# Two head pairs' start-up work put in another order: the first pair's maxima, their turn and two scores ahead of the second pair's join, casts and maxima, with six filling products instead of sixteen

## The chip, the cores and the metric

The kernel runs on one core of one Trainium2 chip. The metric is the device time of one execution in microseconds (us); less is better. A core has five engines that run side by side and wait for each other through semaphores: TensorE (PE in the profile, with PEld for its weight loads), VectorE (DVE), ScalarE (ACT), GpSimd (POOL) and SyncE (SP), which issues the transfers (DMA).

## The reference, cut to what matters

```python
q_rot, k_rot = (rotate(q), rotate(k))            # 8 batches, 8 heads, 576 rows, 64 columns
scores = scale * np.matmul(q_rot, k_rot.transpose(0, 1, 3, 2))
scores = scores - np.max(scores, axis=-1, keepdims=True)
attn = np.exp(scores)
attn = attn / (np.sum(attn, axis=-1, keepdims=True) + 1e-09)
x = np.matmul(attn, v)                           # heads side by side: 4608 x 512
logits = x @ phi                                 # a soft mixture of 8 experts, 32 slots, follows
...
```

Attention for 64 heads comes first; its output goes through a mixture of experts in which every slot is a softmax-weighted mean over all rows. The change touches attention alone.

## The kernel before

**Pairs.** Two heads make a pair, `p` or `q` in the code, and there are 32. For each pair the same steps are run, and each step has a name:

- `load0.p`, `load1.p`: transfers of the pair's q and k into a tile `x_in`, of which there are two. `spin0.p`, `spin1.p` (L237, POOL): products with cosine and sine. `join.p` (L244, DVE): the sum that ends the rotation.
- `high1.p`, `high0.p` (L250, ACT): casts of the rotated k and q to 16 bits, into the tile `hl`; `low.p` (L254, DVE): what the cast left over, also 16 bits. `low.p` is the last reader of the pair's `x_in`, so `load0.p+2`, which uses the same buffer, waits for it.
- the maxima: `m00.p` to `m31.p` are eight units of two products each of the casts (L296, PE), each into a PSUM bank, with a row maximum behind it (L298, DVE); `m_rem.p` is the ninth (L305 and L307). A unit of pair 0 has two more products, which only keep PE busy (L293). `m_min.p` (L320 and L322, DVE) joins the two halves.
- the turn: for pairs 0 and 1, `m_rows.p` is `m_lay` (L346 and L348, PE: six products with an identity matrix, then L349, ACT, which writes the row `peak`). Later pairs do it with transfers.
- the scores: `t0.p` to `t7.p` (L372, PE: eight products, the last two of which subtract `peak`; then L373, ACT: the exponential), `t8.p` for the rest, and `av0.p` to `av4.p` (L407, PE), which multiply by v.

**Banks.** Four double banks of PSUM (`s_ps0` to `s_ps3`) go round. A step takes the one that was given back longest ago; its first product waits until DVE or ACT has read what lay there.

**Order.** Every engine runs its instructions in the order in which the program issues them. At the start of the kernel that order is written out by hand, in a list of names `FRONT`; behind it come tables of times. Ahead of `FRONT` pair 0's rotation, its casts and 21 filling products (`heat`, L724) are issued. `heat.0` in `FRONT` is one more run of 16 filling products; they read the casts of pair 0, go into a bank that nobody reads, and serve only to keep PE busy.

Of the kernel before, what the change touches and what calls it, by code (L numbers as in the profile page):

```python
# [84 lines left out]
    3.879855, 5.365764), "bs3": 34.500363, "bs4": 35.968859, "bs5": 43.198227, "bs6": 50.043832,  # L85
}
FRONT = (
# [70 lines left out]
def attn_softmoe(ctx, tc, qk, v, phi, w1, w2, cs, ident, sel, seg, out):  # L158
# [109 lines left out]
    def bank2(k=None):  # L268
        if k is None:
            k = min((i for i in range(N_S) if age[i] is not None), key=lambda i: age[i])  # L270
        age[k] = None
        t = ps[k].tile([P, 2, 512], F32, name=f"s_ps{k}")
        held[id(t)] = k, t
        return t

    def free(t):
        k, _ = held.pop(id(t))
        age[k] = next(ages)
# [441 lines left out]
    def heat(n):  # L720
        cold = bank2()
        free(cold)
        for _ in range(n):
            nc.tensor.matmul(cold[:, 0, 0:HC], lhsT=lift, rhs=halves[0][:, KH, 0:HC], start=True, stop=True)  # L724

    def small_loads(p):
# [1 line left out]
        nc.sync.dma_start(out=sel_sb, in_=sel)  # L728

    plan.update({  # L730
        "heat": lambda p: heat(16),
        "small_loads": small_loads,
        "join0": lambda p: join(p, 0),
        "join1": lambda p: join(p, 1),
# [332 lines left out]
```

## Time and profile before

| | |
|---|---|
| median of 3 runs | 479.99 us (479.64 to 480.94) |
| the profiled execution's own time | 480.02 us |
| its span, first to last instruction | 478.2 us |
| busy: PE, PEld, DVE, ACT, POOL | 96%, 78%, 77%, 60%, 60% |
| mean granted clock of TensorE | 0.993 |

Every time below is counted from the start of the span. A busy share is a mean over the whole span; the change lies in the first 30 us, so the stretch from 14 to 28 us has to be read by itself. PE's records are pipelined and overlap: the distance from one start to the next tells more than a duration. [...]

### The profile page before, as it was taken

To read this page: it belongs to the slowest core of one execution; us is meant where nothing else is said; L and a number is where in the kernel's file an instruction comes from. 1 tells how busy PE (TensorE), PEld (TensorE's weight loads), DVE (VectorE), ACT (ScalarE), POOL (GpSimd) and SP (SyncE) were. 2 spreads that over 40 slices of the span, in tenths; PEclk is the share of its full clock that TensorE was granted. 3 is DMA by queue.
4 is the path that set the end of the run, shared out by engine and by line. 5 is a ranking of instruction groups with operands and counts; after the bars stand their busy time and mean duration, and the time that the engine had idled before them with its cause. 6 is when DMAs were issued, how large, how long until landed. Compare 5 with 4: busy or idle time off the path is not lost.

```text
span 478.2 us, 24158 instructions
## 1 busy us (share of the span) xinstructions
PE 458.3 (96%) x10787; PEld 371.5 (78%) x10787; DVE 366.3 (77%) x616; ACT 285.7 (60%) x656; POOL 288.0 (60%) x319
## 2 busy tenths in 40 slices
PE   4799999999999999999999999999999999989993
PEld 2487888878888888878887888888888888853762
DVE  5989998888878887998899789988896864263242
ACT  2156767675667567657765676577766766530242
POOL 4886958848783888488856886687749302120000
PEclk9899999999999999999999999999999999999998
DMA  7444845473655355446533653346352044799997
GB/s 280 172 166 176 269 153 197 164 261 102 202 175 213 110 201 174 120 145 210 171 113 123 250 172 125 149 139 217 126 191 112 15 181 163 237 382 407 408 370 319
DMA packets 28795, 93.97 MB, mean 196 GB/s; under 512 B 5012, under 2 KB 5396, under 8 KB 28692
## 3 DMA queue, kind: packets, MB, share of 16 engines
q1 hardware_dynamic: 28692, 92.44, 54.1%
q8 instruction: 84, 1.38, 1.2%
q14 instruction: 19, 0.16, 0.1%
HBM read 82.92 MB, written 9.44 MB: 193 GB/s over the span
## 4 chain that ended last, share of the span: by engine, by line
PE 91%; DVE 4%; ACT 2%; DMA 1%; issue 1%; SPq 0%; DVEq 0%; ACTq 0%
PE s_ps L407 33%; PE s_ps L372 26%; PE s_ps L296 8%; PE s_ps L387 4%; PE o_ps L927 3%; PE o_ps L903 3%; PE s_ps L480 2%; PE s_ps L517 2%; PE c_ps L950 2%; DVE nm L298 2%; PE s_ps L724 2%; PE s_ps L305 2%; PE s_ps L577 1%; DVE hl L254 1%; DMA x_in<-in_qk 1%
## 5 line engine op out<-in xcount | busy, mean ns | idle before, releaser
L237 POOL TENSOR_TENSOR x_in<-x_in,cs_sb 128x288 f32<-128x288 f32 x248 | 236.2, 986 | 79.5 <-DMA x_in<-in_qk 62.5
L298 DVE TENSOR_REDUCE nm<-s_ps 128x2 f32<-128x576 f32 x256 | 187.3, 752 | 50.0 <-PE s_ps L296 48.8
L407 PEld LDWEIGHTS s_ps<-v_in,a_t 128*64 128x64 f32 x4608 | 139.3, 137 | 12.4 <-issue 4.8
L373 ACT ACTIVATE a_t<-s_ps 128x576 f32<-128x576 f32 x256 | 146.0, 658 | 3.6 <-PE s_ps L372 3.1
L407 PE MATMUL s_ps<-v_in,a_t 128*64 128x66 f32 x4608 | 146.4, 222 | 0.2 <-issue 0.2
L372 PE MATMUL s_ps<-hl 64*128 64x288 f16 x1536 | 133.1, 283 | 0.4 <-DVE nm L307 0.2
L372 PEld LDWEIGHTS <-hl 64*128 64x128 f16 x1536 | 79.3, 94 | 18.5 <-issue 8.0
L372 PE MATMUL s_ps<-peak,lift 64*128 64x288 f16 x512 | 75.3, 283 | 0.3 <-ACT peak L349 0.3
L296 PE MATMUL s_ps<-hl 64*128 64x288 f16 x512 | 66.8, 286 | 0.7 <-ACT a_t L373 0.4
L438 ACT COPY o_sb<-s_ps 128x528 f32<-128x528 f32 x31 | 18.6, 601 | 74.9 <-PE s_ps L407 74.9
L456 POOL TENSOR_TENSOR xn<-o_sb,rr 128x640 f32<-128x640 f32 x31 | 41.0, 1332 | 31.7 <-PE s_ps L577 13.9
L254 DVE TENSOR_TENSOR hl<-x_in,hl 128x1152 f16<-128x1152 f32 x32 | 53.7, 1678 | 1.6 <-ACT hl L250 1.6
L250 ACT CAST hl<-x_in 128x576 f16<-128x576 f32 (+1 forms) x66 | 40.9, 659 | 20.5 <-DVE x_in L244 20.4
L244 DVE TENSOR_TENSOR x_in<-x_in 128x1152 f32<-128x1152 f32 (+1 forms) x35 | 46.2, 1321 | 0.1
L296 PEld LDWEIGHTS <-hl 64*128 64x128 f16 x512 | 29.0, 94 | 15.6 <-issue 6.8
L372 PEld LDWEIGHTS <-lift 64*128 64x128 f16 x512 | 27.0, 94 | 4.9 <-issue 0.5
L407 PE MATMUL s_ps<-v_in,a_tr 64*64 64x66 f32 x1152 | 26.4, 224 | 0.0
L307 DVE TENSOR_REDUCE nm<-s_ps 128x2 f32<-128x576 f32 x32 | 24.0, 749 | 2.5 <-PE s_ps L305 2.5
L407 PEld LDWEIGHTS s_ps<-v_in,a_tr 64*64 64x64 f32 x1152 | 21.9, 133 | 4.3 <-issue 3.5
L387 PE MATMUL s_ps<-hl 64*64 64x256 f16 (+1 forms) x384 | 23.9, 286 | 0.0
L962 DVE COPY w_exp<-c_ps 128x512 f32<-128x512 f32 x16 | 10.3, 686 | 17.3 <-PE c_ps L950 14.6
L500 ACT COPY xt<-s_ps 128x576 f32<-128x576 f32 x31 | 19.2, 650 | 5.0 <-PE s_ps L480 5.0
(174 smaller groups left out, 409.2 us busy)
## 6 DMA issues: line engine op xcount, KB each, us to landing
x_in<-in_qk SPq DMA_DIRECT2D x61, 576.0 KB
w_exp<-in_w SPq DMA_DIRECT2D x53, 512.0 KB
v_in<-in_v SPq DMA_DIRECT2D x32, 330.0 KB
out<-w_exp SPq DMA_DIRECT2D x18, 512.0 KB
wt<-in_w SPq DMA_DIRECT2D x11, 512.0 KB
peak<-mr SPq DMA_DIRECT2D x120, 0.5 KB
x_in<-in_qk SPq DMA_DIRECT2D x4, 288.0 KB
cs_sb<-in_cs SPq DMA_DIRECT2D x2, 288.0 KB
```

Of the source, the lines that this page charges most:

```text
L237: eng.tensor_tensor(out=run_on(x[:, c]), in0=run_on(x[:, c]), in1=run_on(cs_sb[:, c]), op=ALU.mult)
L244: nc.vector.tensor_tensor(out=x[:, :, 0], in0=x[:, :, 0], in1=x[:, :, 1], op=ALU.add)
L250: nc.scalar.copy(out=out, in_=loaded[p][:, t, c, 0])
L254: nc.vector.tensor_tensor(out=hl[:, 0:4:3], in0=x[:, :, :, 0], in1=hl[:, 1:3], op=ALU.subtract)
L296: nc.tensor.matmul(s[c, h, 0:HC], lhsT=hl[rows[h], QH, P * j + c.start:P * j + c.stop], rhs=hl[rows[h], KH, half[n]], start=True, stop=True)
L298: nc.vector.tensor_reduce(out=nm[:, n, j:8:4], in_=s[:, :, 0:HC], axis=AX.X, op=ALU.max, negate=True)
L307: nc.vector.tensor_reduce(out=nm[:, :, 8], in_=s[:, :, 0:HC], axis=AX.X, op=ALU.max, negate=True)
L372: nc.tensor.matmul(s[c, h, 0:HC], lhsT=lhs, rhs=rhs, start=(x == 0), stop=(x == 3))
L373: nc.scalar.activation(out=ats[p, b][:, :, half[n]], in_=s[:, :, 0:HC], func=AF.Exp, scale=SCALE)
L387: nc.tensor.matmul(s[rows[h ^ n], n, 0:w] if n else s[rows[h], 0, 512 - w:512], lhsT=lhs, rhs=rhs, start=(x == 0), stop=(x == 3))
L407: nc.tensor.matmul(o[rows[c], h, VW * u:VW * u + VW], lhsT=lhs, rhs=v, start=(i == 0 and u == 0), stop=(left_av[p] == 0 and u == 3 + (c == ...
L456: eng.tensor_tensor(out=xn, in0=t[:, :, :, 0:64], in1=rr.unsqueeze(3).broadcast_to([P, 2, 5, 64]), op=ALU.mult)
```

## The change

In `FRONT` the steps `join.1` and `high1.1` move behind `m_min.0`, `heat.0` and `m_rows.0`, together with `high0.1` and `bs1.2` (which issues nothing at this place), and `t5.0`, `t7.0` move ahead of `m30.1` and `m11.1`. The number of products in `heat.0` goes from 16 to 6.

```diff
-    "logits.0 m11.0 m31.0 low.0 m00.0 spin0.1 spin1.1 m30.0 m20.0 m21.0 m10.0 join.1 m_rem.0 m01.0 load0.2 "
-    "high1.1 m_min.0 heat.0 high0.1 bs1.2 m30.1 m11.1 spin0.2 m_rows.0 low.1 t5.0 t7.0 weights.7 m31.1 t4.0 "
+    "logits.0 m11.0 m31.0 low.0 m00.0 spin0.1 spin1.1 m30.0 m20.0 m21.0 m10.0 m_rem.0 m01.0 load0.2 "
+    "m_min.0 heat.0 m_rows.0 join.1 high1.1 high0.1 bs1.2 t5.0 t7.0 m30.1 m11.1 spin0.2 low.1 weights.7 m31.1 t4.0 "
...
-        "heat": lambda p: heat(16),
+        "heat": lambda p: heat(6),
```

Behind this place `FRONT` goes on as before: `load_v.1 load1.2 t6.0 m20.1 t1.0 m21.1 spin1.2 load0.3 m10.1 join.2 t0.0 t3.0 ...`. The orders of POOL and SP are the same in both.

ACT's queue, from the end of pair 0's casts to the first exponentials (`hl_151` is pair 0's, `x_in_143` pair 1's), before:

```order
L250 CAST hl_151<-x_in_136 128x288 x4
L250 CAST hl_245<-x_in_143 128x576 x2
L349 ACTIVATE peak0_105<-s_ps2_280 128x576
L373 ACTIVATE a_t_289<-s_ps3_290 128x2x288
L373 ACTIVATE a_t_300<-s_ps0_301 128x2x288
```

and with the change:

```order
L250 CAST hl_151<-x_in_136 128x288 x4
L349 ACTIVATE peak0_105<-s_ps0_253 128x576
L250 CAST hl_262<-x_in_143 128x576 x2
L373 ACTIVATE a_t_265<-s_ps1_266 128x2x288
L373 ACTIVATE a_t_276<-s_ps2_277 128x2x288
```

`peak` of pair 0 now stands ahead of the two casts of pair 1.

DVE's queue, from the last of pair 0's plain maxima (into `nm2_184`) to pair 1's third (pair 1's are `nm2_267` before, `nm2_287` with the change), before:

```order
L298 TENSOR_REDUCE nm2_184<-s_ps0_224 128x2
L244 TENSOR_TENSOR x_in_143<-x_in_143 128x8x144
L307 TENSOR_REDUCE nm2_184<-s_ps1_231 128x2
L298 TENSOR_REDUCE nm2_184<-s_ps2_237 128x2
L320 TENSOR_REDUCE cn_sb_114<-nm2_184 128x2x4
L322 TENSOR_REDUCE cn_sb_114<-nm2_184 128x2
L298 TENSOR_REDUCE nm2_267<-s_ps0_268 128x2
L298 TENSOR_REDUCE nm2_267<-s_ps1_272 128x2
L254 TENSOR_TENSOR hl_245<-x_in_143,hl_245 128x2x576
L298 TENSOR_REDUCE nm2_267<-s_ps1_313 128x2
```

and with the change:

```order
L298 TENSOR_REDUCE nm2_184<-s_ps0_224 128x2
L307 TENSOR_REDUCE nm2_184<-s_ps1_230 128x2
L298 TENSOR_REDUCE nm2_184<-s_ps2_236 128x2
L320 TENSOR_REDUCE cn_sb_114<-nm2_184 128x2x4
L322 TENSOR_REDUCE cn_sb_114<-nm2_184 128x2
L244 TENSOR_TENSOR x_in_143<-x_in_143 128x8x144
L298 TENSOR_REDUCE nm2_287<-s_ps3_288 128x2
L298 TENSOR_REDUCE nm2_287<-s_ps0_292 128x2
L254 TENSOR_TENSOR hl_262<-x_in_143,hl_262 128x2x576
L298 TENSOR_REDUCE nm2_287<-s_ps1_303 128x2
```

The join (L244) moved behind the last maxima of pair 0 and their minima; nothing else moved.

PE's queue with the change, one row of each step, from the filling products to `t1.0` (weight loads and a step's other products are left out; the row into `s_ps1_303` is `m31.1`, the last is `t1.0`):

```order
L724 MATMUL s_ps3_246<-hl_151,lift_101 128x288
...
L346 MATMUL s_ps0_253<-id_sb_96,cn_sb_114 128x128 x4
...
L372 MATMUL s_ps1_266<-hl_151 128x288
...
L372 MATMUL s_ps2_277<-hl_151 128x288
...
L296 MATMUL s_ps3_288<-hl_262 128x288
...
L296 MATMUL s_ps0_292<-hl_262 128x288
...
L296 MATMUL s_ps1_303<-hl_262 128x288
...
L372 MATMUL s_ps2_307<-hl_151 128x288
...
L372 MATMUL s_ps3_320<-hl_151 128x288
...
L296 MATMUL s_ps0_330<-hl_262 128x288
...
L372 MATMUL s_ps1_335<-hl_151 128x288
```

Before, the two rows into `s_ps3_288` and `s_ps0_292` (`m30.1` and `m11.1`) stood ahead of the turn (L346). Behind `m31.1` the order is the same in both, and in both `t1.0` goes into the bank that `m31.1` used (`s_ps1`).

## Rows read from the trace of the kernel before

**Rows 1.** The page: busy time of each engine (part 1), chain by engine (part 4).
```profile
PE 458.3 (96%) x10787; PEld 371.5 (78%) x10787; DVE 366.3 (77%) x616; ACT 285.7 (60%) x656; POOL 288.0 (60%) x319
...
PE 91%; DVE 4%; ACT 2%; DMA 1%; issue 1%; SPq 0%; DVEq 0%; ACTq 0%
```

**Rows 2.** Waits of PE from 46 to 420 us: total us, times, longest.
```profile
PE s_ps L372 <- DVE nm L307: 0.2, 1, 0.2
```

**Rows 3.** Timeline of PE, 17 to 28 us: start, us, what, [idle before].
```profile
17.14 3.65 PE L724 MATMUL s_ps<-hl,lift 128*128 128x288 f16 x16 [0.24 <-DVE nm L298]
20.71 0.52 PE L296 MATMUL s_ps<-hl 64*128 64x288 f16 x4
21.16 1.16 PE L346 MATMUL s_ps<-id_sb,cn_sb 128*128 128x128 f32 x8
...
23.33 0.30 PE L372 MATMUL s_ps<-peak,lift 64*128 64x288 f16 x2 [0.27 <-ACT peak L349]
...
23.94 0.30 PE L296 MATMUL s_ps<-hl 64*128 64x288 f16 x2
...
25.16 0.55 PE L372 MATMUL s_ps<-hl 64*128 64x288 f16 x6
...
26.68 0.55 PE L372 MATMUL s_ps<-hl 64*128 64x288 f16 x6
```

**Rows 4.** Timeline of DVE, 14 to 25.5 us.
```profile
14.35 3.40 DVE L298 TENSOR_REDUCE nm<-s_ps 128x2 f32<-128x576 f32 x5
17.67 1.34 DVE L244 TENSOR_TENSOR x_in<-x_in 128x1152 f32<-128x1152 f32 x1
18.94 0.74 DVE L307 TENSOR_REDUCE nm<-s_ps 128x2 f32<-128x576 f32 x1
19.60 0.74 DVE L298 TENSOR_REDUCE nm<-s_ps 128x2 f32<-128x576 f32 x1
...
20.47 0.15 DVE L322 TENSOR_REDUCE cn_sb<-nm 128x2 f32<-128x4 f32 x1
21.15 1.42 DVE L298 TENSOR_REDUCE nm<-s_ps 128x2 f32<-128x576 f32 x2 [0.53 <-PE s_ps L296]
22.49 1.58 DVE L254 TENSOR_TENSOR hl<-x_in,hl 128x1152 f16<-128x1152 f32 x1
24.28 0.76 DVE L298 TENSOR_REDUCE nm<-s_ps 128x2 f32<-128x576 f32 x1 [0.21 <-PE s_ps L296]
```

**Rows 5.** Timeline of ACT, 18.5 to 25 us.
```profile
19.05 1.24 ACT L250 CAST hl<-x_in 128x576 f16<-128x576 f32 x2 [7.53 <-DVE x_in L244]
22.63 0.65 ACT L349 ACTIVATE peak<-s_ps 128x576 f16<-128x576 f32 x1 [2.34 <-PE s_ps L348]
23.66 1.75 ACT L373 ACTIVATE a_t<-s_ps 128x576 f32<-128x576 f32 x3 [0.39 <-PE s_ps L372]
```

**Rows 6.** PE by window: stretch, length, PE busy (instructions), granted clock, DMA share, GB/s.
```profile
14.10:17.10 3.00, 1.28 (x12) 1.00 0.56 161
17.54:20.94 3.40, 3.40 (x18) 0.50 0.99 387
20.95:23.00 2.05, 2.05 (x22) 1.00 0.16 57
```

**Rows 7.** Timeline of SP's queue: issues of `x_in` transfers, 13 to 36 us.
```profile
15.77 9.17 SPq L232 DMA_DIRECT2D x_in<-in_qk  x3
```

**Rows 8.** Timeline of POOL, 13 to 40 us: the products of pair 3.
```profile
28.04 7.76 POOL L237 TENSOR_TENSOR x_in<-x_in,cs_sb 128x288 f32<-128x288 f32 x8 [1.81 <-DMA x_in<-in_qk]
```

**Rows 9.** Timeline of DVE, 36 to 43.7 us: the join of pair 3, and a wait.
```profile
37.11 1.35 DVE L244 TENSOR_TENSOR x_in<-x_in 128x1152 f32<-128x1152 f32 x1
...
41.16 0.17 DVE L326 TENSOR_REDUCE min<-nm 128x9 f32<-128x18 f32 x1
41.49 1.92 DVE L254 TENSOR_TENSOR hl<-x_in,hl 128x1152 f16<-128x1152 f32 x1 [0.16 <-ACT hl L250]
43.34 0.20 DVE L334 STREAM_TRANSPOSE turned<-min 128x32 f32<-128x32 f32 x1
```

## The prediction

> **What bounds the kernel now.** I read the page first. PE is busy for 96% of the span, and the chain of work that ended last runs over PE for 91% [rows 1]. Busy PE records overlap and prove little alone, so next I asked what PE waits for once the start is over: between 46 and 420 us there are just two waits in the list, of 0.2 us each (the other is a wait for issue) [rows 2]. So PE has no reserve there that could take up a delay. What PE loses or gains before 30 us should stand in the end time, and the question is only when PE gets through the stretch that the change rearranges.
>
> There I read the three timelines side by side. PE runs 16 filling products from 17.14 until `m30.1` follows at 20.71, then turns pair 0's maxima (L346) at 21.16, and `t1.0` comes at 25.16 [rows 3]. DVE has hardly any gap: five maxima until 17.67, the join of pair 1, the last two maxima of pair 0, the minima, 0.53 idle, then two maxima of pair 1 and `low.1` until 24.07, and the maximum of `m31.1` at 24.28 [rows 4]. ACT makes pair 1's casts from 19.05 to 20.29, then idles for 2.34 until the turn is done [rows 5]. The reader should see two chains: PE to ACT to PE (turn, `peak`, scores) for pair 0, and DVE to ACT to PE to DVE (join, casts, products, maxima, `low.1`) for pair 1. They meet at the bank of `m31.1`, which `t1.0` takes next. Its maximum ends at 24.28 + 0.76 = 25.04, and `t1.0` starts at 25.16 [rows 3, 4]: pair 1's chain has about 0.1 us to spare.
>
> [...]
>
> **The change part by part.**
>
> *The turn comes earlier.* Nothing changes on DVE until 17.67. Without the join there, the maximum of `m_rem.0` starts at 17.67, that of `m01.0` 0.66 later (19.60 - 18.94), at 18.33, and the second minimum 0.87 after it (20.47 - 19.60), from 19.20 to 19.35 [rows 4]. Handing over to PE takes about 0.05, as from `peak` (22.63 + 0.65 = 23.28) to 23.33 [rows 3, 5]. So the turn starts at 19.40 instead of 21.16.
>
> *Ten fills go.* Sixteen took 20.71 - 17.14 = 3.57, or 0.22 each; six end at about 18.5 [rows 3]. PE then waits 0.9 us for the minima, so these ten cost or give nothing by themselves: what is late next is the turn's input.
>
> *The turn at the lower clock.* From the turn's first product to `peak` it took 22.63 - 21.16 = 1.47 at a granted clock of 1.00 [rows 3, 5, 6]. At 19.40 the clock stands at 0.50 if it falls and rises as before; PE's work ahead of 17 us is the same. Then 1.54 us until 20.94 do half as much, 0.77, and 0.70 remain: `peak` starts at 21.64 and ends at 22.29. Bounds: 20.87 for its start with a full clock throughout, 22.34 with half throughout. The first I call 0.77 early, the second 0.70 late.
>
> *The casts wait behind `peak`.* The join now starts at about 19.28 and ends at 20.62 (1.34 long) [rows 4]. ACT is free then, and casts followed the join within 0.05 before (17.67 + 1.34 = 19.01, and 19.05) [rows 4, 5]. But `peak` stands ahead of them in ACT's queue. ACT starts one instruction of this size 0.55 after another ((1.75 - 0.65) / 2), so the casts start at 21.64 + 0.55 = 22.19, and end 1.24 later, at 23.43 [rows 5]. This is the new wait: 1.5 us in which ACT holds ready work.
>
> That the queue doesn't let a ready instruction pass is shown on DVE: a minimum ended at 41.16 + 0.17 = 41.33, the transpose that reads only it ran at 43.34, behind a `low` that waited for ACT [rows 9]. [...]
>
> *Pair 1's chain.* `m30.1` then starts at 23.48 and its maximum 0.34 later (23.94 to 24.28 for `m31.1`), at 23.82, against 21.15 before [rows 3, 4]. DVE idles for 3.2 us instead of 0.53. Two maxima and `low.1` take until 24.07 - 0.07 (DVE starts the next some 0.07 before an end: 17.67 + 1.34 against 18.94), so 2.85; `m31.1`'s maximum runs from 26.67 to 27.43, and `t1.0` starts at 27.48 instead of 25.16: 2.3 us late [rows 3, 4]. The two scores done early don't help: PE reaches `t1.0` and stands still.
>
> *What may be won back.* From `m31.1` to `t1.0` PE took 25.16 - 23.94 = 1.22 for two units and two scores, and 26.68 - 25.16 = 1.52 for the next two units and two scores, so 0.30 there was waiting [rows 3]; ACT's exponentials are earlier now, but `t3.0` must wait for `t1.0`'s. Between 0 and 0.3 comes back; I take 0.1, as its bank is the nearer wait.
>
> *SP and POOL.* `low.1` frees the tile for `load0.3`, which SP holds among the three issues from 15.77 to 24.94 [rows 7]. It comes 2.67 later, and POOL's products of pair 3 with it: they end at 38.5 instead of 28.04 + 7.76 = 35.80 [rows 8]. `join.3` started at 37.11 and would now be due at 39.3, so this is covered by 0.8 [rows 9]. Uncovered, it would cost 0.45.
>
> **Sum:** +2.3 - 0.1 = +2.2 us. From the profiled execution's own 480.02 us (the median of the runs is 479.99, practically the same) that is **482.2 us**, +0.46%. A change of 0.3% (1.44 us) is about what a measurement of this kernel can tell from none. With the clock's bounds: 481.4 to 482.9.
>
> **The rivals.**
>
> *The clock falls again* (slower still). PE gets `m31.1` at about 24.0 (after the first exponential), two scores and a unit until about 25.7, and then stands until 27.48: some 1.5 us of work in 4. The clock fell before after 1.28 of 3.00 [rows 6]. If it is at 0.50 for 3.40 us again, at most half of that is lost, 1.7; part of it lies behind DVE, so 1.1: 483.3, at most 483.9. For more than 0.20 I would need a second such stretch in the rows. Chance 0.20.
>
> *The clock doesn't fall before the turn.* Then +1.4, 481.4, at the edge of what can be told. The runs of before lie 1.3 us apart, so executions differ. Against it: PE's work ahead is unchanged. Chance 0.13.
>
> *The delay is taken up later.* 480.0. [...] Chance 0.06.
>
> *ACT runs the casts first.* They would end at 20.66 + 1.24 = 21.90, maxima start at 22.29 instead of 23.82, `t1.0` is 0.8 late: 480.8. Chance 0.02, by rows 9.
>
> *Faster.* Pair 0's chain alone decides: the turn starts 1.76 earlier, so 478.3. It holds if `t1.0` isn't held by `m31.1`'s bank; for that the casts must end 2.3 us earlier than I find, by 21.1, which is before `peak` is even written. For it: the ten fills are gone from the engine that bounds the kernel. Chance 0.06.
>
> **How the numbers follow.** The forecast (481.6 to 482.9) has 0.50; 0.03 is for what I don't see. Forecast, second fall and full clock hold 0.83, so the range is 480.9 to 484.0: a half us below 481.4 for the sizes, and up to the bound of the second fall. Slower by over 0.3%: 0.50 + 0.20 + half of 0.13 = 0.77. Within: 0.065 + 0.06 + 0.02 + 0.015 = 0.16. Faster: 0.07.
>
> **What would show it.** In the changed kernel: L346 at about 19.4; `peak` (L349) at 21 to 22, with two L250 casts straight behind it; an idle time of DVE of about 3 us ahead of pair 1's first maxima, which start near 23.8; PE idle for 1.5 us or more ahead of `t1.0`, with DVE's maximum as its releaser; `load0.3` issued near 26.7. After that the same rows as before, 2.2 later, to the end. I am wrong if the casts run ahead of `peak`, if `t1.0` doesn't wait for DVE, if the shift shrinks between 30 and 420 us, or if the clock in 17 to 28 us is another.

## The result and the profile after

The changed kernel took 483.77 us in the median (481.05 to 494.23, 20 runs), the kernel before 480.54 us (479.52 to 486.69, 20 runs). The medians count every run, the ratios here undisturbed runs alone (13 of the changed kernel's 20), so a ratio is not the quotient of the medians beside it. The ratio is 1.0054 (95% interval 1.0036 to 1.0073): the change made the kernel slower by about 2.6 us (0.0054 x 480.5). The profiled execution took 481.51 us, 1.5 more than that of before.

The page of the changed kernel, busy times and the chain that ended last, beside [rows 1]:

```profile
PE 458.1 (95%) x10777; PEld 370.1 (77%) x10777; DVE 367.8 (77%) x616; ACT 285.9 (60%) x656; POOL 289.1 (60%) x319
...
PE 92%; DVE 4%; ACT 1%; issue 1%; DMA 1%; SPq 0%; DVEq 0%; ACTq 0%
```

Nothing moves here: ten products fewer on PE, and the span is 1.5 us longer. The stretch of the change has to be opened. The timeline of PE, 17 to 28 us, beside [rows 3] (start, us, what, idle before it and what ended that):

```profile
17.20 1.60 PE L724 MATMUL s_ps<-hl,lift 128*128 128x288 f16 x6
19.52 1.13 PE L346 MATMUL s_ps<-id_sb,cn_sb 128*128 128x128 f32 x8 [0.72 <-PE s_ps L724]
...
21.66 0.30 PE L372 MATMUL s_ps<-peak,lift 64*128 64x288 f16 x2 [0.27 <-ACT peak L349]
...
22.79 0.85 PE L296 MATMUL s_ps<-hl 64*128 64x288 f16 x6 [0.35 <-ACT hl L250]
23.88 0.55 PE L372 MATMUL s_ps<-hl 64*128 64x288 f16 x6 [0.24 <-ACT a_t L373]
...
26.63 0.54 PE L372 MATMUL s_ps<-hl 64*128 64x288 f16 x6 [1.46 <-DVE nm L298]
```

The turn (L346) starts at 19.52 instead of 21.16 and the scores of pair 0 come earlier, but `t1.0`, the last row, stands still for 1.46 us until DVE has read a bank, and comes at 26.63 instead of 25.16. The timelines of DVE (14 to 27.5 us) and ACT (18.5 to 25 us) show why, beside [rows 4, 5]:

```profile
18.39 0.74 DVE L298 TENSOR_REDUCE nm<-s_ps 128x2 f32<-128x576 f32 x1
...
19.42 1.61 DVE L244 TENSOR_TENSOR x_in<-x_in 128x1152 f32<-128x1152 f32 x1
23.13 1.42 DVE L298 TENSOR_REDUCE nm<-s_ps 128x2 f32<-128x576 f32 x2 [2.10 <-PE s_ps L296]
24.47 1.43 DVE L254 TENSOR_TENSOR hl<-x_in,hl 128x1152 f16<-128x1152 f32 x1
25.83 1.41 DVE L298 TENSOR_REDUCE nm<-s_ps 128x2 f32<-128x576 f32 x2
```
```profile
20.96 0.65 ACT L349 ACTIVATE peak<-s_ps 128x576 f16<-128x576 f32 x1 [9.38 <-PE s_ps L348]
21.50 1.23 ACT L250 CAST hl<-x_in 128x576 f16<-128x576 f32 x2
```

Pair 1's join (L244) starts at 19.42 instead of 17.67. The casts run behind `peak`, at 21.50, 0.43 after the 21.07 at which they could have (19.42 + 1.61, and 0.04 as in [rows 4, 5]). The first maxima of pair 1 start at 23.13 instead of 21.15, after 2.10 us in which DVE had nothing to do; then `low.1` holds DVE, and only the first maximum of the row at 25.83 frees the bank of `m31.1` for `t1.0`.

PE's granted clock in this execution (1.00 is full speed), by window, beside [rows 6] (us, PE busy, PEld, DVE, ACT, POOL, granted clock, DMA share, GB/s):

```profile
15.32:18.73 3.41, 3.33 (x18) 1.27 (x14) 3.41 (x6) 0.00 (x0) 2.51 (x4) 0.50 0.93 322
18.74:20.94 2.20, 1.48 (x15) 1.26 (x16) 2.09 (x4) 0.00 (x0) 2.20 (x3) 1.00 1.01 399
```

It fell to 0.50 all the same, but from 15.32 to 18.73 where the execution of before had 17.54 to 20.94 [rows 6], and was back at 1.00 when the turn began, at 19.52. For the turn that comes to the same as the rival "the clock doesn't fall before the turn", for which the prediction gave 481.4; the profile took 481.51.

Is the delay kept? PE's waits for DVE between 46 and 420 us (total, times, longest), beside [rows 2]:

```profile
PE s_ps L372 <- DVE nm L307: 0.3, 1, 0.3
```

There is still no reserve to take it up. It even grows: the exponentials of the scores are 1.3 us later than before at 28 us and 1.9 later at 50. In between stands the join of pair 3; the timelines of DVE (36 to 43.7 us) and POOL (13 to 40 us), beside [rows 8, 9]:

```profile
38.46 1.92 DVE L244 TENSOR_TENSOR x_in<-x_in 128x1152 f32<-128x1152 f32 x1
```
```profile
38.38 2.66 POOL L237 TENSOR_TENSOR x_in<-x_in,cs_sb 128x288 f32<-128x288 f32 x2 [1.13 <-DMA x_in<-in_qk]
```

The join takes 1.92 instead of 1.35. POOL has just begun its next product; before, it was idle from 35.80 to 37.70, when the join began at 37.11. In six profiles with the new order's parts this join takes 1.74 to 1.95, and there the lateness grows by 0.42 to 0.63 between 28 and 50 us; in three (`low.1` behind `m31.1`, 13 fills, and six fills in the old order with extra fills, all described below) it takes 1.35, and the lateness does not grow. The two kernels with a late `low.1` are left out of this, since PE waits elsewhere too there.

From 50 to 129 us the exponentials stay 1.9 late. From 138 to 200 they are 1.5 late, at 300 us 1.7, and the end is 1.5 later. The step at 129 to 138 us is one of the execution of before: six other profiles read below come 0.5 us nearer to it at the same place.

### The profile page after: what moved, and what is told of

Read it like the earlier page. It is cut to its first block, busy times and chain, and to the rows that moved or that the text cites. A ratio compares the mean times of both kernels' runs of the same rounds, so it can differ in the third digit from the quotient of the medians.

```text
span 479.7 us, 24139 instructions
## 1 busy us (share of the span) xinstructions
PE 458.1 (95%) x10777; PEld 370.1 (77%) x10777; DVE 367.8 (77%) x616; ACT 285.9 (60%) x656; POOL 289.1 (60%) x319
## 4 chain that ended last, share of the span: by engine, by line
PE 92%; DVE 4%; ACT 1%; issue 1%; DMA 1%; SPq 0%; DVEq 0%; ACTq 0%
PE s_ps L407 34%; PE s_ps L372 26%; PE s_ps L296 8%; PE s_ps L387 4%; PE o_ps L927 3%; PE o_ps L903 3%; PE s_ps L517 2%; PE c_ps L950 2%; PE s_ps L480 2%; PE s_ps L305 2%; PE s_ps L724 1%; DVE nm L298 1%; PE s_ps L577 1%; DVE hl L254 1%; DMA x_in<-in_qk 1%
## 5 line engine op out<-in xcount | busy, mean ns | idle before, releaser
L237 POOL TENSOR_TENSOR x_in<-x_in,cs_sb 128x288 f32<-128x288 f32 x248 | 237.3, 990 | 79.6 <-DMA x_in<-in_qk 68.7
L298 DVE TENSOR_REDUCE nm<-s_ps 128x2 f32<-128x576 f32 x256 | 187.4, 752 | 49.8 <-PE s_ps L296 48.5
L372 PE MATMUL s_ps<-hl 64*128 64x288 f16 x1536 | 133.3, 283 | 2.2 <-DVE nm L298 1.6
L372 PEld LDWEIGHTS <-hl 64*128 64x128 f16 x1536 | 79.2, 94 | 21.4 <-issue 11.1
L372 PE MATMUL s_ps<-peak,lift 64*128 64x288 f16 x512 | 75.3, 283 | 0.3 <-ACT peak L349 0.3
L254 DVE TENSOR_TENSOR hl<-x_in,hl 128x1152 f16<-128x1152 f32 x32 | 52.4, 1639 | 1.5 <-ACT hl L250 1.4
L244 DVE TENSOR_TENSOR x_in<-x_in 128x1152 f32<-128x1152 f32 (+1 forms) x35 | 49.3, 1409 | 0.1
L372 PEld LDWEIGHTS <-lift 64*128 64x128 f16 x512 | 27.1, 94 | 4.8 <-issue 0.5
```

The costliest lines, as they stand in the source:

```text
L237: eng.tensor_tensor(out=run_on(x[:, c]), in0=run_on(x[:, c]), in1=run_on(cs_sb[:, c]), op=ALU.mult)
L244: nc.vector.tensor_tensor(out=x[:, :, 0], in0=x[:, :, 0], in1=x[:, :, 1], op=ALU.add)
L254: nc.vector.tensor_tensor(out=hl[:, 0:4:3], in0=x[:, :, :, 0], in1=hl[:, 1:3], op=ALU.subtract)
L298: nc.vector.tensor_reduce(out=nm[:, n, j:8:4], in_=s[:, :, 0:HC], axis=AX.X, op=ALU.max, negate=True)
L372: nc.tensor.matmul(s[c, h, 0:HC], lhsT=lhs, rhs=rhs, start=(x == 0), stop=(x == 3))
```

## The experiments

Four kernels were compared with before in one batch (480.09 us there), four in a second (479.63), four in a third (479.83). "Old order" is `FRONT` of before, "new order" that of the changed kernel.

### The fills alone: six and 13 in the old order, 16 in the new

The change has two parts, so each was made alone.

```diff
# e2: old order          # e12: old order         # e1: new order
-  heat(16)              -  heat(16)              -  heat(6)
+  heat(6)               +  heat(13)              +  heat(16)
```

> The old order with 6 filling products; nothing of the result is left out. Order theory: no slower than before, 479.6 to 480.2, since m30.1 can start at the end of the casts (20.3) and no longer waits for the fills (20.7): 0.4 us to win at most. Fills theory: slower by 1.5 to 2.6 us, 481.5 to 483, with a lower mean granted clock than 0.993 in many executions.

> The order of before with 13 fills in place of 16. In the trace of before 16 end at 20.7, and pair 1's casts at 20.3; 13 at the same clock end at about 20.05. If only what PE has to do ahead of m30.1 counts: m30.1 at 20.3, first maximum of pair 1 0.36 earlier, the turn 0.3 earlier, the end 0 to 0.3 earlier: ratio 0.9995 to 1.000. If PE's unbroken work up to the casts is what brings the clock back to 1.00 in time: the same here, since the gap is 0.25 us at most, while six fills (a gap of 1.6) cost 0.3 to 0.4%. A ratio of 1.003 or more would say that the number of fills matters by something else than the gap.

> The new order with all 16 filling products; nothing of the result is left out. Order theory (ACT holds pair 1's casts behind the row peak, DVE idles, t1.0 waits for the bank of m31.1): still slower than before, by 1.5 to 2.9 us, 481.5 to 482.9, since the fills now also stand ahead of the turn; pair 1's first maximum starts at 23 us or later and t1.0 waits for DVE. Fills theory (the ten products that went were what kept TensorE's clock up, and the order costs nothing): as before, 480.0.

| kernel | median us | ratio to before | 95% interval |
|---|---|---|---|
| old order, 6 fills | 482.49 | 1.0031 | 1.0013 to 1.0050 |
| old order, 13 fills | 479.86 | 1.0009 | 0.9991 to 1.0027 |
| new order, 16 fills | 483.09 | 1.0076 | 1.0049 to 1.0104 |
| new order, 6 fills (the change) | 483.77 | 1.0054 | 1.0036 to 1.0073 |

Three fills fewer cost nothing that can be measured; ten fewer cost 0.31% in the old order, 1.5 us (0.0031 x 480). So neither theory holds alone: against the one the fills cost something in the old order, against the other the order costs 0.76% with all 16 fills. The two intervals of the new order overlap, so that the fills' number makes no measured difference there: 16 fills lasted until 21.03 in its profile, at a clock of 0.50 from 14.88 to 21.70, and held the turn up to that time, so that `t1.0` came at 28.30. The profile of the old order with six fills is of an execution far above its median (488.87 us), so its rows are not read; the same two parts come again below.

### The casts ahead of the turn, and fills in the new stall

In the first kernel the join and the casts of pair 1 stay behind pair 0's minima, but go ahead of `m_rows.0`, and `m30.1`, `m11.1` ahead of `t5.0`, `t7.0`. The second puts nine more filling products ahead of `t1.0`, into the bank that `m21.1` takes next.

```diff
# e3, against the changed kernel
-  m_min.0 heat.0 m_rows.0 join.1 high1.1 high0.1 bs1.2 t5.0 t7.0 m30.1 m11.1
+  m_min.0 heat.0 join.1 high1.1 high0.1 m_rows.0 bs1.2 m30.1 m11.1 t5.0 t7.0
# e4, against the changed kernel
-  t6.0 m20.1 t1.0 m21.1
+  t6.0 m20.1 hot.0 t1.0 m21.1
...
+        "hot": lambda p: hot(9),
```

> The changed kernel, but with the casts of pair 1 ahead of the row peak in ACT's queue and m30.1, m11.1 ahead of the first two scores; the join stays behind the minima. Nothing of the result is left out. Order theory: pair 1's first maximum at about 22.2 instead of 23.1, t1.0 at about 25.9 instead of 26.6: half of the loss is gone, 480.4 to 481.0. If the cast queue doesn't matter and the join's place alone costs: as the changed kernel, 481.5 at the best.

> The changed kernel with nine more filling products just ahead of t1.0, into the bank that m21.1 uses next, where PE stands idle for 1.46 us; nothing of the result is left out. Order theory: the best executions stay at 481.0 to 481.5, since t1.0 still waits for the maximum of m31.1. Clock theory (the idle time ahead of t1.0 is what lets the clock fall in many executions): the median falls from 483.1 to about 481.5 and executions lie within 1.5 us. If the clock falls for another reason, the median stays near 483.

The casts ahead missed: 484.52 us, ratio 1.0092 (1.0058 to 1.0125). In its profile the clock was at 0.50 from 14.93 to 28.58 and the turn took 2.04 us (20.12); pair 1's first maxima came at 23.60, but `t1.0` only at 27.91, behind PE's other work at the low clock. Fills in the stall gave 483.21, 1.0053 (1.0033 to 1.0073), the ratio of the change, which is what was expected if the clock falls for another reason than the stall: it was low long before, from 14.78 to 25.02. Up to 26 us this second kernel runs the changed kernel's instructions, so its profile shows that kernel with a clock of 0.50 during the turn: `peak` at 22.13, casts at 22.68, and then, on DVE and PE (22 to 30 and 25 to 30 us), the first maxima at 24.50 and `t1.0` at 27.91, 2.75 later than before:

```profile
24.50 1.43 DVE L298 TENSOR_REDUCE nm<-s_ps 128x2 f32<-128x576 f32 x2 [3.21 <-PE s_ps L296]
```
```profile
27.91 0.54 PE L372 MATMUL s_ps<-hl 64*128 64x288 f16 x6 [0.18 <-DVE nm L298]
```

Its exponentials are 3.1 late at 50 us, against 1.9 in the changed kernel's own profile: the difference is about what the low clock in the turn adds.

### Extra fills to hold the clock at 1.00: old and new order

In four kernels 25 short filling products (128 by 224) were put between the last units of pair 0, into unused columns of the units' own banks, meant to leave PE no lull at 14 to 17 us.

```diff
+    def warm_up(s, n):
+        for _ in range(n):
+            nc.tensor.matmul(s[:, 0, HC:512], lhsT=lift, rhs=halves[0][:, KH, 0:512 - HC], start=True, stop=True)
...
+        if p == 0:
+            warm_up(s, (0, 0, 0, 0, 0, 17, 3, 3)[len(beat) - 1])
...
+            warm_up(s, 2)
# e5: old order, heat(26)   e8: old order, heat(6)
# e6: new order, heat(16)   e7: e3's order, heat(16)
```

> The kernel before with 25 small filling products in the gaps between pair 0's maxima (17 of them in the gap of 13.4 to 15.1) and 26 instead of 16 in heat.0, so that PE is never idle for long ahead of pair 1's maxima; nothing of the result is left out. Clock theory: no fall of the granted clock near 15 to 25 us, 0.99 or more in all executions, and 479.3 to 480.0, 0 to 0.7 us faster than before. If the clock falls for another reason: as before, 480.0, or slower where the fills run at the lower clock.

> The kernel before with the fills in the gaps but only 6 in heat.0; nothing of the result is left out. PE is then idle from about 18 to 20.3. If it is the emptiness just behind the fills that lowers the clock: slower than the old order with 26 fills by 0.5 to 2 us, with a lower clock between 20 and 26. If the gap of 13.4 to 15.1 alone decides: the same as with 26 fills, 479.3 to 480.0.

> The changed kernel with the same small filling products in the gaps and 16 in heat.0; nothing of the result is left out. Order theory: with the clock held, the order alone still costs 1.4 to 1.6 us, 481.3 to 481.6, and executions lie closer together than those of the changed kernel (median 483.1). Fills theory alone (the order costs nothing): the same time as the old order with these fills.

> The changed kernel with the fills in the gaps, 16 in heat.0, and with pair 1's casts ahead of the row peak and m30.1, m11.1 ahead of the first two scores; nothing of the result is left out. Queue theory (ACT's queue is a part of the order's price): 0.4 us faster than the new order with the same fills, first maximum of pair 1 at about 22.7. If only the join's place counts: the same time as the new order with the same fills.

| kernel | median us | ratio to before | 95% interval |
|---|---|---|---|
| old order, extra fills, `heat(26)` | 488.06 | 1.0147 | 1.0119 to 1.0175 |
| old order, extra fills, `heat(6)` | 482.28 | 1.0040 | 1.0020 to 1.0060 |
| new order, extra fills, `heat(16)` | 485.41 | 1.0098 | 1.0069 to 1.0127 |
| casts ahead, extra fills, `heat(16)` | 483.45 | 1.0079 | 1.0056 to 1.0102 |

In the profiles of the two kernels with the new order's parts the clock was held (0.995 in the mean; 1.00 from 11.50 us to 475.40 with the new order). In that of the old order with six fills it fell all the same, at 21.23, and the means of the four kernels' executions reach from 0.978 to 0.996. No kernel became faster, and all four expected times were missed. The old order with 26 fills is even the slowest, and its one profile is of an execution far above its median (493.65 us): why it loses stays open. The whole times of these four therefore can't size the order; the starts of the other three profiles can (lines are numbered a little higher there: L304 is L298 of the other kernels, L354 L346, L380 L372).

New order, held: ACT, 17 to 27 us, and PE's row of `t1.0`:

```profile
21.15 0.65 ACT L357 ACTIVATE peak<-s_ps 128x576 f16<-128x576 f32 x1 [9.38 <-PE s_ps L356]
21.70 1.23 ACT L250 CAST hl<-x_in 128x576 f16<-128x576 f32 x2
```
```profile
27.09 0.55 PE L380 MATMUL s_ps<-hl 64*128 64x288 f16 x6 [1.74 <-DVE nm L304]
```

Casts ahead, held, the same two:

```profile
21.12 1.25 ACT L250 CAST hl<-x_in 128x576 f16<-128x576 f32 x2 [9.24 <-DVE x_in L244]
22.27 0.64 ACT L357 ACTIVATE peak<-s_ps 128x576 f16<-128x576 f32 x1
```
```profile
26.68 0.54 PE L380 MATMUL s_ps<-hl 64*128 64x288 f16 x6 [1.17 <-DVE nm L304]
```

Without any fall of the clock the new order still brings `t1.0` 1.93 late (27.09 against 25.16), so the clock is not the cause of all of the order's part. Letting the casts run ahead of `peak` makes them 0.58 earlier, the first maxima 0.57 earlier (22.76 against 23.33; 22.7 was expected), and `t1.0` 0.41. That is the share of ACT's queue; most of the rest was there when the casts could start, since the join ran at 19.73 instead of 17.67.

The old order with the extra fills and `heat(6)` shows what ten missing fills do. Its PE timeline, 17 to 26 us, and its clock by window:

```profile
17.44 0.90 PE L732 MATMUL s_ps<-hl,lift 128*128 128x288 f16 x6
20.58 0.42 PE L300 MATMUL s_ps<-hl 64*128 64x288 f16 x4 [2.25 <-DVE nm L304]
21.05 1.89 PE L354 MATMUL s_ps<-id_sb,cn_sb 128*128 128x128 f32 x8
```
```profile
11.00:21.20 10.20, 7.12 (x68) 4.22 (x67) 9.86 (x15) 1.68 (x3) 9.04 (x10) 1.00 0.57 210
21.25:24.60 3.35, 3.35 (x24) 2.49 (x25) 2.36 (x3) 0.69 (x2) 3.23 (x4) 0.50 0.04 15
```

PE stood idle for 2.25 us until 20.58, the granted clock was 0.50 from 21.25 to 24.60, and the turn (L354) took 1.89 instead of 1.16 [rows 3]; the exponentials are 1.0 us late from 27 to 126 us, although the first maxima (20.92) are earlier than before.

### The bank: `low.1` behind the maximum of `m31.1`

If `t1.0` waits because DVE reads `m31.1`'s bank only behind `low.1`, then moving `low.1` must remove that wait. One kernel moves it behind `m31.1`, one behind `m10.1` (with `load0.3`, which waits for it), and one does the second in the old order.

```diff
# e9, against the changed kernel
-  spin0.2 low.1 weights.7 m31.1 t4.0
+  spin0.2 weights.7 m31.1 low.1 t4.0
# e10, against the changed kernel; e11 the same against the old order
-  spin0.2 low.1 weights.7 m31.1 ... spin1.2 load0.3 m10.1 join.2
+  spin0.2 weights.7 m31.1 ... spin1.2 m10.1 low.1 load0.3 join.2
```

> The new order with its six fills; only low.1 moves on DVE, behind the maximum of m31.1. The bank theory (t1.0 stands still because DVE reads m31.1's bank only after low.1): m31.1's maximum starts some 1.4 us earlier, at about 24.5, and t1.0 comes at 25.2 to 25.3 instead of 26.63, if the clock is at 1.00 during the turn as in the changed kernel's profile. The next to wait is the score that takes m20.1's bank (t0.0), for 0.6 to 0.9 us, so that the exponentials at 28 to 30 us are 0.6 to 0.9 later than before instead of 1.4, and the median is some 0.6 below the changed kernel's 483.8: ratio 1.003 to 1.004. The rival, that the loss lies in the casts behind peak alone: t1.0 still waits for something else and stays near 26.6; ratio 1.005.

> The new order with its six fills; low.1 moves behind the maxima of m31.1, m20.1, m21.1 and m10.1, and load0.3, which waits for it, behind it on SP. The bank theory: t1.0 at about 25.2, no wait of PE over 0.4 us for DVE between 22 and 28 us, exponentials at 28 us within 0.3 of before; load0.3 comes some 2 us later than in the changed kernel, join.3 with it by about 0.8, which may cost up to that. Best executions 479.7 to 480.7, against 481.05 of the changed kernel. What the lower granted clock adds in many executions (about 1.1 in the median) should stay: median 480.8 to 481.8, ratio 1.001 to 1.004. The rival (casts alone): 1.005.

> Control: the order of before with its 16 fills, low.1 and load0.3 moved as in the run before. In the trace of before t1.0 has 0.1 us to spare against m31.1's bank, so there is next to nothing to win: t1.0 25.0 to 25.2, ratio 0.999 to 1.001 if load0.3's 2 us are covered, up to 1.003 if pair 3's join isn't. If the late low.1 helps both orders alike (by 0.3% or more), the bank has nothing to do with the new order.

The first kernel: 483.19 us, 1.0077 (1.0053 to 1.0100). Its timelines of DVE, 17 to 30 us, ACT, 17 to 30 us, and PE, 25 to 30 us:

```profile
19.53 1.75 DVE L244 TENSOR_TENSOR x_in<-x_in 128x1152 f32<-128x1152 f32 x1
24.50 2.09 DVE L298 TENSOR_REDUCE nm<-s_ps 128x2 f32<-128x576 f32 x3 [3.22 <-PE s_ps L296]
26.50 1.35 DVE L254 TENSOR_TENSOR hl<-x_in,hl 128x1152 f16<-128x1152 f32 x1
```
```profile
22.14 0.65 ACT L349 ACTIVATE peak<-s_ps 128x576 f16<-128x576 f32 x1 [10.44 <-PE s_ps L348]
22.68 1.23 ACT L250 CAST hl<-x_in 128x576 f16<-128x576 f32 x2
```
```profile
26.64 0.55 PE L372 MATMUL s_ps<-hl 64*128 64x288 f16 x6 [0.30 <-DVE nm L298]
28.57 0.54 PE L372 MATMUL s_ps<-hl 64*128 64x288 f16 x6 [1.02 <-DVE nm L298]
```

Its clock was at 0.50 from 14.54 to 24.78, as in the kernel with fills in the stall (14.78 to 25.02), and in both the first maxima start at 24.50; these two profiles can be compared. `t1.0` came at 26.64 instead of 27.91, with a wait of 0.30, and the next score, `t0.0`, then waited 1.02 for the bank of `m20.1`. So the wait is the bank's, and it hangs on the place in DVE's queue, as said; moving one step only hands it on: at 28 us the exponentials are 2.4 late instead of 2.6. The ratio of 1.003 to 1.004 that went with it was missed; the mean clock of its executions was 0.984 to 0.990.

Behind `m10.1` the wait ahead of `t1.0` is gone. PE, 17 to 30 us:

```profile
26.52 0.55 PE L372 MATMUL s_ps<-hl 64*128 64x288 f16 x6
```

The clock was at 0.50 here too, from 16.69 to 23.52, and `t1.0` did not reach the 25.2 that I expected, but the exponentials are 1.2 late at 28 us, where they are 2.6 late with fills in the stall. So the bank's wait was worth 1.4 us there. The whole time doesn't show it: the kernel took 486.26 us, 1.0140 (1.0112 to 1.0168), and the control in the old order 485.34, 1.0104 (1.0084 to 1.0125), both missed. In the control everything is on time at 28 us. At 30.71 PE waits 0.96 for a maximum that now stands behind `low.1`, which makes the exponentials 1.2 late at 39 us, and then the join of pair 3 is late. DVE, 36 to 45 us, and PE, 39 to 45 us:

```profile
39.88 1.93 DVE L244 TENSOR_TENSOR x_in<-x_in 128x1152 f32<-128x1152 f32 x1 [1.51 <-POOL x_in L237]
```
```profile
42.54 0.85 PE L372 MATMUL s_ps<-hl 64*128 64x288 f16 x6 [1.76 <-DVE nm L298]
43.15 0.48 PE L372 MATMUL s_ps<-peak,lift 64*128 64x288 f16 x2
```

`load0.3` left SP at 29.60 instead of 24.94, POOL's products of pair 3 came from 32.66, the join waited 1.51 for them, PE then 1.76 for DVE, and the clock fell to 0.50 (42.64 to 46.05). The exponentials are on time at 27 us and 5.1 late at 63. What I had priced at up to 0.3% cost 1%: the late `low.1` costs PE two waits and a fall of the clock, not the late transfer's excess alone.

## Why the prediction was right

It forecast slower, 482.2 us within 480.9 to 484.0, and the time was 483.77, with a ratio that means 2.6 us where it had 2.2. The direction was right, and so was the mechanism: `t1.0` waits for the bank of `m31.1`. That the size came so near is partly luck. In the profiled execution `t1.0` was 1.47 late and not 2.3, since the clock in 17 to 28 us was another (one of the prediction's signs of being wrong), and 0.57 came on top at pair 3's join, which the sum doesn't have. The median is above the forecast's 482.9, in the part of the range kept for a second fall of the clock, which the profile doesn't show; 0.5 us of the excess is that the kernel before took 480.54 here and not the 480.02 from which the sum starts. Point by point:

- **The turn comes earlier** (19.40 forecast): 19.52. Right.
- **Ten fills cost nothing by themselves.** This is the term that was mis-sized. In the changed kernel's one profile PE had 0.72 us of slack there, and it cost nothing. Over executions, six fills in the old order cost 1.5 us (ratio 1.0031) and 13 cost none. The profiles read here say with what it goes: with 13 or 16 fills the granted clock was back at 1.00 at 18.74 to 21.70 (four kernels without the extra fills), with six at 18.73 in the changed kernel, and at 23.52, 24.78, 25.02 and 28.58 in four others with the new order's parts; in four of these five, then, after the turn. One profile for each kernel is no distribution, and that the median's rest comes from it is argued, not shown; in the new order 16 fills were no faster than six.
- **The turn at the lower clock** (`peak` at 21.64, bounds 20.87 and 22.34): 20.96 in the profile, at full clock, and 22.13 to 22.20 in the three profiles in which it was at 0.50 throughout with this order. The chosen middle occurred in none; both bounds held.
- **The casts wait behind `peak`, 1.5 us**: no run shows this size. It was 0.43 in the profile, 1.36 where the clock was low (22.68 against 19.53 + 1.75 + 0.04, in the kernel with `low.1` behind `m31.1`). The size hangs on the clock, and at full clock 1.5 was over three times too much. The casts-ahead pair at a held clock gives 0.58. That ACT's queue doesn't let ready work pass was carried over from DVE's [rows 9]; it is shown where the clock was low: the casts' data were there at 21.28 (19.53 + 1.75), ACT did nothing until `peak` began at 22.14, and the casts ran behind it, at 22.68. In the changed kernel's profile `peak` had begun at 20.96, before the casts' data were there (21.03), so that ACT was simply busy.
- **Pair 1's chain**: first maxima 23.82 forecast, 23.13 measured; `t1.0` +2.3 forecast, +1.47 measured, +2.75 with the clock low (with half throughout the prediction's own bound is +3.0 there, 2.3 + 0.70). Of the 1.98 by which the first maxima were late, 1.75 is the join's later start, 0.27 its longer run (1.61 against 1.34), 0.43 the casts behind `peak`; 0.47 went back, 0.37 of it because `m30.1` no longer waits for fills (it started at 20.71, with its casts done at 20.29 and 0.05 for the hand-over [rows 3, 5]). From there to `t1.0` another 0.5 went back: `low.1` ran 0.15 shorter (1.43 against 1.58), `m31.1`'s maximum no longer waited for PE (0.21 [rows 4]), and the 0.1 to spare was used up.
- **What may be won back**, 0.1: `t3.0` came at 28.03 against 26.68, 1.35 late, so 0.12 there. Right.
- **SP and POOL, covered by 0.8**: `load0.3` left SP at 26.78 (15.83 + 10.95; 26.7 was forecast), and pair 3's join at 38.46 had no wait. So far right, and the control shows a price where the cover is gone. But the later transfers moved POOL's next products too, and the join, which met one of them, took 0.57 longer. The prediction put this at nothing; it is most of the step from 1.3 to 1.9.
- **The delay taken up later**: refuted: 1.5 us lost at 26 us were still missing at the end, as PE's waits from 46 to 420 us (0.3 us in all) had it.
- **The clock falls again**: not seen in the changed kernel's profile, where PE ran at 1.00 from 18.73 to 476 despite the stall at 25.2. Of the other executions only the mean clock is known, 0.973 to 0.994.

So the wait for `m31.1`'s bank is shown, and with it the first 1.3 to 1.5 us: where it was taken away, 1.4 of 2.6 us were gone at 28 us. That pair 3's join adds the next 0.6 is read from nine profiles and was not tried by itself. The ratio's 2.6 lies between the 1.9 of the changed kernel's profile at 50 us and the 3.1 with the clock low in the turn; that the other executions lie between them for the clock's sake is argued. No experiment took the loss out of the whole time, and no kernel tried here is measurably faster than before; 13 fills in the old order equal it.

## What to carry to other kernels

When a step is moved ahead of another on one engine, follow the step that was passed: what hangs on it can be later by more than the length of what passed it (here pair 1's join by 1.75 us, its first maxima by 1.98), since each queue that it crosses can hold it too (its casts 0.43 behind `peak`), and its last reader may own the buffer that the favoured chain needs next (`t1.0` stood still for 1.46). Filling products can be worth more than the time that they occupy, and this may show only over many executions (ten fewer cost 1.5 us in the old order, three fewer nothing that can be measured): price them by a run with fewer and one with slightly fewer. A covered transfer has an edge; find out how far it is before leaning on it (with `load0.3` issued at 26.78 pair 3's join had no wait, with 29.60 it waited 1.51), and what else the later transfer moves: here it moved another engine's work into the way of a step that had no wait.

## What the hardware did that was not expected

- The stretch at a granted clock of 0.50 near the start began at another time in each profiled execution: 17.53 us before, 15.32 with the change, 14.54 to 16.69 in the seven other profiles read of kernels without extra fills, though PE's work up to 17 us is the same in all of them.
- A clock of 1.00 (from 10.00 to 476.90 us in the profile of the casts-ahead kernel with extra filling products) was no gain: that kernel had means of 0.990 to 0.996 and took 482.68 to 485.10, while the changed kernel took 481.30 to 482.64 at 0.993 and 0.994. What these executions lose, and where, stays open.
- Pair 1's join on DVE took 1.34 us before, 1.61 to 1.78 in the six kernels of the new order without extra fills, and 1.36 in the two with them. The traces go with one reason: a product of POOL (L237) that is under way when the join starts. In the changed kernel one such product ran from 19.02 to 19.81, so that 0.39 of it was left when the join started at 19.42, and the join was 0.27 longer; the product behind it took 1.91 instead of 0.79. With `low.1` behind `m31.1` 0.53 was left and the join 0.41 longer; before, POOL had nothing under way. Each of the 18 joins and `low` steps from 14 to 60 us in the profiles of before and of the change took, within 0.08, 1.35 plus what was left of POOL's product beyond 0.13. No run tried it by moving POOL's work.
